# Loading and splitting a guessed first expert's weights during attention

## Chip, core and metric

One core of a Trainium2 chip runs the whole program. The metric is device time in microseconds, the median of three runs of one launch.

## What is computed

Three layers in a row, all in float32. First attention: 4 batches, 8 heads, 576 positions, 64 channels a head; the first four heads see a window of 32, the others every fourth of 128 positions. Its output, seen as 2304 tokens of 512 channels, goes through a layer of 8 experts of which each token takes one (the largest logit, with a bias that depends on the token's modality). Then comes a dense layer with a squared ReLU.

```python
logits = x @ w_gate + modality_bias[modality_id]
e_idx = np.argmax(logits, axis=1)
for e in range(E):
    mask = e_idx == e
    h = np.maximum(x[mask] @ w1[e], 0.0)
    out[mask] = gate_w[mask, None] * (h @ w2[e])
...
h = np.maximum(x @ w_in, 0.0)
return h * h @ w_out
```

w1 is 512 x 1024 and w2 1024 x 512 for each expert, 2 MB each.

## The kernel before

**Attention** runs in 48 units of 96 queries and four heads (`schedule`, the loop over i). A unit passes through steps in several rounds of the loop: A (line 321) writes a mask and the scores into one of PSUM banks 0 to 2 (lines 335, 338) and VectorE (DVE) takes the maximum; C takes the exponential on ScalarE (ACT, line 350); two rounds later D transposes (line 360) and ACT copies (pt); one round later F multiplies by v (line 374), DVE makes x, and SyncE's queue (SP) stores it to the DRAM tensor xd; two rounds later H transposes x (line 413), and ACT and DVE split it into a high and a low part (xth, xtl). After twelve units, one batch is done: its gate logits (line 434) and `route` and `select`, some sixty small DVE operations that count tokens per expert, are threaded into the following rounds as the generator `side`, step by step.

**Experts** run in slots of 128 tokens of one expert (`Moe`). Every float32 product is made of three TensorE (PE) products of rounded parts (float32r): high by high, high by low, low by high. So weights have to be split: ACT copies the staged weights st into the high part (w1h, w2h) and DVE subtracts for the low part (w1l, w2l). A slot j has `begin` (load its expert number and flag into registers, gather its tokens from xd by Pool), `tx` (four transposes into the bank that l1 uses next, xh and xl), `l1` (24 matmuls of 128x512), `th` (eight transposes of the hidden layer, hth and htl) and `l2` (24 matmuls). `main(j)` issues l1(j), then prep(j + 1) if that slot has begun, then l2(j - 1), then th(j). From slot 1 on, loading (line 708) and splitting (line 727) are conditional: they happen only where a slot's expert differs from that of the slot before. Slot 0 loads and splits always (lines 710 and 722 to 726); Pool does two of its w1 subtractions, and the w2 split is threaded into its l1.

**What sets the order.** `slots(0, 6)` is a filler: each round of the attention loop takes three microseconds' worth of steps by nominal costs from it, and a step that yields a negative number ends a round's share. `ready` is how many slots have been selected: 2 after batch 1, 6 after batch 2, all after batch 3 (`WAVES`). If slot j has not been prepared when its turn comes, the filler passes six times (2 x `GAP`, two a round) before it prepares it. The order within an engine is the order of issue; engines wait for each other by semaphores. After slot 5 the rest of the slots run with the decoding of the dense layer's weights beside them, then the dense layer.

Line 785 of the changed kernel is 761 of this one (l1), 815 is 791 (l2), 798 is 774 (th), 771 is 747 (tx), 451 is 434, 468 is 451, 430 is 413, 377 is 360, 391 is 374, 352 and 355 are 335 and 338, 750 is 727.

Of the kernel before, what the change touches and what calls it, by code (L numbers as in the profile page):

```python
# [63 lines left out]
@with_exitstack  # L64
def body(ctx, tc, ins, out):
    nc = tc.nc
    const = ctx.enter_context(tc.tile_pool(name="const", bufs=1))
    dram = ctx.enter_context(tc.tile_pool(name="dram", bufs=1, space=bass.MemoryType.DRAM))
    psum = ctx.enter_context(tc.tile_pool(name="psum", bufs=1, space=PSUM))
    g = Ctx()  # L70
    g.tc, g.nc, g.ins, g.out = tc, nc, ins, out
    g.xd = dram.tile([NT, XW], F32, name="xd")
    g.ya = dram.tile([NA * 128, XW], F32, name="ya")
    g.yb = dram.tile([NT - NA * 128 + 128, XW], F32, name="yb")
    g.wod = [dram.tile([NE, 128, DM], F32, name=f"wo{i}") for i in range(2)]
    g.bk = [psum.tile([128, 512], F32, name=f"bk{i}") for i in range(8)]
    g.ident = const.tile([128, 128], F32, name="ident")
    g.iota = const.tile([128, NCOL], F32, name="iota")
    g.esel = const.tile([1, 4, NSLOT], I32, name="esel")
    g.nsl = const.tile([1, 1], I32, name="nsl")  # L80

    with ExitStack() as mctx:
        moe = Moe(g, mctx)
        with ExitStack() as actx:
            att = Attention(g, actx)
            att.warm(9)
            with tc.manual_schedule():
                schedule(g, att, moe)
        ffn = Ffn(g, ctx)
        with tc.manual_schedule():  # L90
            for cost in moe.slots(NA, NTT):
                if cost == MARK:
                    ffn.side()
            ffn.rest()
            moe.extras()
            moe.tag()
            ffn.l1(0, 0)
            ffn.l1(0, 1)
            run(moe.l2(NSLOT - 1))
        mctx.close()  # L100
        ffn.run()
# [6 lines left out]
def run(steps):  # L108
    for _ in steps:
        pass  # L110


def schedule(g, att, moe):
    nu = B * UPB
    moe.banks((2, 4), (4, 2), (2, 2), (7, 7))
    side, fc, sc, hold, nxt, due = None, 0.0, 0.0, 0, 0, 0
    early = None
    i = 0
    fill, more = moe.slots(0, NA), True

    def step(cost):
        nonlocal side, sc, hold
        if i < hold:
            return
        sc += cost
        while side is not None and sc > 0 and i >= hold:
            c = next(side, None)
            if c is None:
                side = None
            elif c == 0:  # L130
                hold, sc = i + 1, 0.0
            else:
                sc -= c
        sc = min(sc, 0.0)

    def one():
        step(0.01 - sc)

    def filler(cost, late):
        nonlocal more, fc  # L140
        fc += cost
        while more and fc > 0:
            c = next(fill, None)
            if c is None:
                more = False
            elif c == -2 and late:
                fc = max(fc, BURST)
            elif c < 0:
                fc = 0.0
            else:  # L150
                fc -= c
                if early and c == MARK:
                    early.step()
        fc = min(fc, 0.0)

    for i in itertools.count():
        att.tail = i >= nu + 2
        ns, no, nh = (2, (5,), (5,)) if att.tail else (2, (5,), (6,)) if moe.ready else (3, (5, 4), (7,))
        r = RATE2 if i >= nu + 5 else RATE1 if moe.prepped else RATE
        if i == nu + 6:  # L160
            att.units.close()
            early = Early(g)
        if i == nu + 2:
            moe.banks((2, 4), (6, 0), (1, 1), (7, 3))
        att.A(i, (0, 1, 2)[:ns])
        if i == SETUP:
            att.setup()
        if NTL < i <= nu + 5 and i % NTL == 5:
            att.logits(i // NTL - 1, 1)
            if moe.ready and not att.tail:  # L170
                no, nh = nh, no
        if i > hold:
            step(r)
        att.H(i - 5, nh)
        filler(FILL / 2, False)
        att.D(i - 2)
        step(r)
        att.F(i - 3, no, one)
        att.C(i)
        filler(FILL / 2, True)  # L180
        step(r)
        if NTL < i <= nu + 5 and i % NTL == 4:
            att.logits(i // NTL - 1, 0)
        if due and side is None:
            moe.ready = sum(WAVES[due - 1])
            moe.pump()
            due = 0
        if nxt < B and side is None and i >= (nxt + 1) * UPB + 5:
            side = att.batch(nxt)
            due, sc, hold = nxt, 0.0, i + 1  # L190
            nxt += 1
        if not more:
            break
    run(side or ())
    early.close()
    if due:
        moe.ready = NSLOT
        moe.pump()


class Attention:
    def __init__(self, g, ctx):
# [25 lines left out]
        self.reset = al.tile([QT, E, TPB], F32, name="reset")  # L228
        self.taken = al.tile([1, E], F32, name="taken")
        self.pref = al.tile([QT, E], F32, name="pref")  # L230
        self.tok = al.tile([QT, TPB], F32, name="tok")
        self.tbl = al.tile([128, NCOL], F32, name="tbl")
        self.g.itab = None
# [22 lines left out]
    def setup(self):  # L256
        g, nc, ac = self.g, self.g.nc, self.ac
        wraw, mb, modi = self.raw
        nc.gpsimd.memset(self.reset, 1.0)
        nc.gpsimd.memset(self.reset[:, :, 0:1], 0.0)  # L260
        nc.gpsimd.memset(self.tbl, 0.0)
        nc.vector.memset(self.ones, 1.0)
        nc.vector.tensor_copy(self.wg[:, :, 0:E], wraw)
        nc.vector.tensor_tensor(out=self.wg[:, :, E:], in0=wraw, in1=self.wg[:, :, 0:E].bitcast(F32), op=ALU.subtract)
        nc.vector.tensor_scalar(out=self.carry, in0=g.iota[:QT, :E], scalar1=float(128 * NTT), scalar2=None, op0=ALU.mult)
        nc.vector.tensor_scalar(out=self.taken, in0=g.iota[0:1, :E], scalar1=float(NTT), scalar2=None, op0=ALU.mult)
        nc.vector.tensor_scalar(out=self.pref, in0=g.iota[:QT, :E], scalar1=-1.0, scalar2=8.0, op0=ALU.mult, op1=ALU.add)
        modf = ac.tile([QT, NI], F32, name="modf")
        nmod = ac.tile([QT, NI], F32, name="nmod")
        btmp = ac.tile([QT, NI, E], F32, name="btmp")  # L270
        nc.vector.tensor_copy(modf, modi[:, :, 0])
        nc.vector.tensor_scalar(out=nmod, in0=modf, scalar1=-1.0, scalar2=1.0, op0=ALU.mult, op1=ALU.add)
        for j, m, t in ((0, nmod, self.bias), (1, modf, btmp)):
            nc.vector.tensor_tensor(
                out=t, in0=mb[:, j:j + 1, :].to_broadcast([QT, NI, E]),
                in1=m.unsqueeze(2).to_broadcast([QT, NI, E]), op=ALU.mult)
        nc.vector.tensor_tensor(out=self.bias, in0=self.bias, in1=btmp, op=ALU.add)

    def bank(self):
        return self.g.bk[5 if self.tail else 6]  # L280
# [292 lines left out]
    def select(self, j0, n):  # L573
# [35 lines left out]
        ef = new([1, NSLOT + 1], "sef")  # L609
        if j0 == 0:  # L610
            yield 0.12
            nc.vector.memset(ef[:, 0:1], -1.0)
        else:
            yield 0.12
            nc.vector.tensor_copy(ef[:, 0:1], self.elast)
# [56 lines left out]
class Moe:  # L672
# [29 lines left out]
    def stage(self, j, w):  # L702
# [1 line left out]
        e, c = self.chg[j][:2]  # L704
        src = self.g.ins["w1" if w == 0 else "w2"]
        src = src[bass.ds(e, 1)].rearrange("o p c f -> p (o c) f")
        if j:
            nc.sync.dma_start(out=self.st[w], in_=src, cond=c, cond_hint=False)
        else:
            nc.sync.dma_start(out=self.st[w], in_=src)  # L710

    def split(self, j, w):
        nc, tc = self.g.nc, self.g.tc
# [1 line left out]
        src, hi, lo = self.st[w], self.wh[w], self.wl[w]  # L715
        n = src.shape[1]

        def part(k, eng=nc.vector):
            nc.scalar.activation(out=hi[:, k, :], in_=src[:, k, :], func=AF.Copy)
            eng.tensor_tensor(out=lo[:, k, :], in0=src[:, k, :], in1=hi[:, k, :].bitcast(F32), op=ALU.subtract)  # L720

        if j == 0:
            for k in range(n):
                part(k, nc.gpsimd if w == 0 and k < 2 else nc.vector)
                yield -1
            return
        with tc.If(c > 0, preferred_fallthrough_block=False):  # L727
            for k in range(n):
                part(k)

    def begin(self, j):
        nc, g = self.g.nc, self.g
# [80 lines left out]
    def prep(self, j):  # L813
# [1 line left out]
        self.prepped = j + 1  # L815
        yield 0.5
        yield -2
        yield from self.split(j, 0)
        self.done[0] = j + 1
        self.pump()  # L820

# [3 lines left out]
    def main(self, j):  # L825
        if j:
            self.tag()
        self.pump()
        w2 = self.split(0, 1) if j == 0 else iter(())
        for c in self.l1(j):  # L830
            next(w2, None)
            yield c
        if self.begun > j + 1:
            yield from self.prep(j + 1)
        yield 0
# [1 line left out]
            yield from self.l2(j - 1)  # L837
        yield from self.th(j)
        yield -2
        yield from self.split(j, 1) if j else w2  # L840
        self.done[1] = j + 1
        self.pump()
        yield 0
# [316 lines left out]
```

## Time and profile before

| | us |
|---|---|
| runs: median (lowest, highest) | 802.98 (801.03, 803.93) |
| the profiled execution, its span | 803.79, 802.0 |
| PE busy, share of the span | 778.8, 97% |
| DVE, ACT, Pool busy | 412.3, 324.5, 168.5 |
| mean granted clock of PE | 0.991 |

A busy PE is not PE at its peak: how fast it goes is read from the distance between the starts of its instructions, and the granted clock tells whether it ran at 2.4 GHz (1.0) or at 1.2 (0.5). The stages in the order of time: attention to about 120 us, its last units with the first slots to about 160, expert slots to about 385, the dense layer to the end. Of the rows below, those of the stretches (busy time of each engine, granted clock, DMA) tell where PE has holes, those in the order of time what each hole waits for.

### The profile page before, as it was taken

How to read it: one execution, taken by the hardware profiler on the slowest of the kernel's cores; microseconds unless marked ns; L12 is line 12 of the kernel's file. 1: busy time of each engine (PE TensorE's matmuls, PEld its weight loads, DVE VectorE, ACT ScalarE, POOL GpSimd, SP SyncE). 2: the span in 40 equal slices, each digit the busy share in tenths (PEclk: the TensorE clock that was granted, in tenths of full speed). 3: DMA queues.
4: the chain of work that ended last, by engine and by line, in shares of the span. 5: the costliest groups of instructions: out<-in, count | busy, mean ns of one | idle time of the engine just before them, and what ended most of it. 6: DMA issues, size and time to landing. Idle time of an engine off the chain costs nothing.

```text
span 802.0 us, 12644 instructions
## 1 busy us (share of the span) xinstructions
PE 778.8 (97%) x4273; PEld 671.3 (84%) x4273; DVE 412.3 (51%) x1136; ACT 324.5 (40%) x779; POOL 168.5 (21%) x222
## 2 busy tenths in 40 slices
PE   8999987999899999999899999999999999999996
PEld 5888875778688888878888899899899998998995
DVE  5787888566447777443279832333243233234232
ACT  4877766333445455543244522322232232232221
POOL 4245632224413333301033510010010001001001
PEclk9999998999999999999999999999999999999999
DMA  7676672234534444361355310010010001001001
GB/s 220 186 166 174 183 256 81 73 93 134 155 108 132 119 134 143 133 198 35 118 167 146 105 40 27 4 50 27 1 52 1 27 14 40 1 0 40 1 1 39
DMA packets 49130, 72.65 MB, mean 91 GB/s; under 512 B 7296, under 2 KB 31712, under 8 KB 48544
## 3 DMA queue, kind: packets, MB, share of 16 engines
q1 hardware_dynamic: 43040, 56.00, 24.1%
q0 software_dynamic: 3280, 10.76, 4.5%
q10 hardware_dynamic: 2736, 4.99, 1.7%
q8 instruction: 35, 0.57, 0.3%
q14 instruction: 39, 0.32, 0.1%
HBM read 132.27 MB, written 17.06 MB: 186 GB/s over the span
## 4 chain that ended last, share of the span: by engine, by line
issue 39%; PE 10%; POOL 2%; POOLq 0%; DVE 0%; ACT 0%; ACTq 0%
PE bk L1010 5%; PE bk L1064 4%; POOL out L1069 2%; PE bk L791 1%; PE bk L993 0%; POOLq L1156 0%; DVE fsq L1020 0%; ACT fr L1018 0%; POOLq L1069 0%; ACTq L1018 0%
## 5 line engine op out<-in xcount | busy, mean ns | idle before, releaser
L1020 DVE TENSOR_TENSOR fsq<-fr 128x384 f32<-128x384 f32 x96 | 53.4, 556 | 162.8 <-ACT fr L1018 162.3
L1010 PE MATMUL bk<-yh,wih 128*128 128x384 f32 x384 | 130.0, 339 | 2.1 <-ACTq L860 1.5
L1010 PE MATMUL bk<-yh,wil 128*128 128x384 f32 x384 | 129.2, 336 | 0.0
L1010 PE MATMUL bk<-yl,wih 128*128 128x384 f32 x384 | 129.0, 336 | 0.0
L1018 ACT ACTIVATE fr<-bk 128x384 f32<-128x384 f32 x96 | 46.9, 488 | 192.0 <-PE bk L1010 191.4
L1064 PE MATMUL bk<-woh,fhh 128*128 128x512 f32 x288 | 113.2, 393 | 0.0
L1064 PE MATMUL bk<-woh,fhl 128*128 128x512 f32 x288 | 112.8, 392 | 0.0
L1064 PE MATMUL bk<-wol,fhh 128*128 128x512 f32 x288 | 112.6, 391 | 0.0
L1069 POOL DMA_INDIRECT out<-fout,fidx x18 | 17.6, 978 | 320.8 <-DVE fout L1068 320.2
L1029 DVE TENSOR_TENSOR fhl<-fsq,fhh 128x384 fp32r<-128x384 f32 x96 | 55.3, 576 | 44.2 <-ACT fhh L1028 44.0
L1010 PEld LDWEIGHTS bk<-yh,wih 128*128 128x128 f32 x384 | 72.2, 188 | 4.8 <-ACTq L860 1.8
L1010 PEld LDWEIGHTS bk<-yl,wih 128*128 128x128 f32 x384 | 72.2, 188 | 1.8
L1010 PEld LDWEIGHTS bk<-yh,wil 128*128 128x128 f32 x384 | 72.2, 188 | 0.0
L1028 ACT ACTIVATE fhh<-fsq 128x384 fp32r<-128x384 f32 x96 | 50.3, 524 | 50.9 <-DVE fsq L1020 50.8
L1064 PEld LDWEIGHTS bk<-woh,fhl 128*128 128x128 f32 x288 | 54.0, 188 | 12.3
L761 PE MATMUL bk<-w1h,xh 128*128 128x512 f32 x152 | 63.4, 417 | 0.8 <-DVE htl L777 0.8
L791 PE MATMUL bk<-w2h,hth 128*128 128x512 f32 x152 | 61.6, 405 | 1.9 <-ACTq L727 1.9
L1064 PEld LDWEIGHTS bk<-wol,fhh 128*128 128x128 f32 x288 | 54.1, 188 | 9.6
L1064 PEld LDWEIGHTS bk<-woh,fhh 128*128 128x128 f32 x288 | 54.1, 188 | 9.5
L761 PE MATMUL bk<-w1l,xh 128*128 128x512 f32 x152 | 61.0, 401 | 0.4 <-DVEq L727 0.4
L761 PE MATMUL bk<-w1h,xl 128*128 128x512 f32 x152 | 60.9, 401 | 0.0
L791 PE MATMUL bk<-w2l,hth 128*128 128x512 f32 x152 | 60.0, 395 | 0.4 <-DVEq L727 0.4
(174 smaller groups left out, 1360.1 us busy)
## 6 DMA issues: line engine op xcount, KB each, us to landing
st<-in_w SPq DMA_DIRECT2D x41, 2048.0 KB
raw<-in_wi SPq DMA_DIRECT2D x32, 256.0 KB
raw<-in_wo SPq DMA_DIRECT2D x32, 256.0 KB
v<-in_v SPq DMA_DIRECT2D x7, 780.0 KB
q<-in_q SPq DMA_DIRECT2D x7, 576.0 KB
kd<-in_k SPq DMA_DIRECT2D x14, 288.0 KB
xd<-x SPq DMA_DIRECT2D x40, 96.0 KB
yb<-y ACTq DMA_DIRECT2D x13, 256.5 KB
```

Source lines behind the costliest of these rows:

```text
L761: nc.tensor.matmul(ps, a[:, c, :], w[:, c, sl], start=k == 0, stop=k == 11)
L791: nc.tensor.matmul(ps, a[:, c, :], w[:, c, :], start=k == 0, stop=k == 23)
L1010: nc.tensor.matmul(ps, w[:, c, f * 128:(f + 1) * 128], a[:, c, :], start=k == 0, stop=k == 11)
L1018: nc.scalar.activation(out=r, in_=ps, func=AF.Relu)
L1020: nc.vector.tensor_tensor(out=s, in0=r, in1=r, op=ALU.mult)
L1028: nc.scalar.activation(out=hh, in_=s, func=AF.Copy)
L1029: nc.vector.tensor_tensor(out=hl, in0=s, in1=hh.bitcast(F32), op=ALU.subtract)
L1064: nc.tensor.matmul(acc[t], a[:, sl], w[:, f, :], start=f == 0 and j == 0, stop=f == NF - 1 and j == 2)
L1069: dma = nc.gpsimd.indirect_dma_start(out=out, out_offset=bass.IndirectOffsetOnAxis(ap=self.idx[:, i:i + 1].bitcast(U32), axis=0), in_=o, i ...
```

## The change

Before attention starts, `setup` makes a guess at slot 0's expert: it marks each modality's largest bias, and takes the lower-numbered of the marked experts (`g.guess`, eight small DVE operations). A generator `first` then loads that expert's w1 and w2 in sixteen pieces of 128 x 512 (256 KB each) by SP; each piece is split two steps later by ACT and DVE into w1h and w1l, w2h and w2l. The attention loop takes a step of it in every second round from round 4, and in each round after the 24th, while no routing step is due. With round 34 it is through. `select` compares slot 0's expert with the guess instead of with -1; loading and splitting of slot 0 are now conditional like those of the others, and the always-path with Pool's two subtractions and the threaded w2 split is gone.

```diff
@@ schedule
+    first = moe.first()
@@
+        if i > SETUP and (side is None or i < hold) and (i % 2 == 0 or i > 2 * UPB):
+            next(first, None)
         if due and side is None:
+            run(first)
             moe.ready = sum(WAVES[due - 1])
             moe.pump()
@@ setup
+        nc.vector.tensor_reduce(out=top, in_=mb[0:1], axis=AX.X, op=ALU.max)
+        nc.vector.tensor_tensor(out=at, in0=mb[0:1], in1=top.to_broadcast([1, 2, E]), op=ALU.is_equal)
+        nc.vector.tensor_tensor(out=at[:, 0], in0=at[:, 0], in1=at[:, 1], op=ALU.max)
+        nc.vector.tensor_tensor_scan(out=cum, data0=at[:, 0], data1=at[:, 0], initial=0.0, op0=ALU.add, op1=ALU.bypass)
+        nc.vector.tensor_scalar(out=at[:, 1], in0=cum, scalar1=0.5, scalar2=None, op0=ALU.is_lt)
+        nc.vector.tensor_reduce(out=self.first, in_=at[:, 1], axis=AX.X, op=ALU.add)
+        nc.vector.tensor_scalar(out=self.first, in0=self.first, scalar1=float(E - 1), scalar2=None, op0=ALU.min)
+        nc.vector.tensor_copy(g.guess, self.first)
@@ select
-            nc.vector.memset(ef[:, 0:1], -1.0)
+            nc.vector.tensor_copy(ef[:, 0:1], self.first)
@@ stage
-        if j:
-            nc.sync.dma_start(out=self.st[w], in_=src, cond=c, cond_hint=False)
-        else:
-            nc.sync.dma_start(out=self.st[w], in_=src)
+        nc.sync.dma_start(out=self.st[w], in_=src, cond=c, cond_hint=False)
+
+    def first(self):
+        nc, ins = self.g.nc, self.g.ins
+        e = nc.values_load(self.g.guess[0:1, 0:1], engines=(ET.SP,), min_val=0, max_val=E - 1)
+        parts = []
+        for w in range(2):
+            st, hi, lo = (x[w].rearrange("p c f -> p (c f)") for x in (self.st, self.wh, self.wl))
+            src = ins["w1" if w == 0 else "w2"][bass.ds(e, 1)].rearrange("o p c f -> p (o c f)")
+            for k in range(8):
+                parts.append([x[:, k * 512:(k + 1) * 512] for x in (st, src, hi, lo)])
+        for i in range(len(parts) + 2):
+            if i < len(parts):
+                nc.sync.dma_start(out=parts[i][0], in_=parts[i][1])
+            if i > 1:
+                st, _, hi, lo = parts[i - 2]
+                nc.scalar.activation(out=hi, in_=st, func=AF.Copy)
+                nc.vector.tensor_tensor(out=lo, in0=st, in1=hi.bitcast(F32), op=ALU.subtract)
+            yield
@@ split
-        if j == 0:
-            for k in range(n):
-                part(k, nc.gpsimd if w == 0 and k < 2 else nc.vector)
-                yield -1
-            return
         with tc.If(c > 0, preferred_fallthrough_block=False):
             for k in range(n):
-                part(k)
+                nc.scalar.activation(out=hi[:, k, :], in_=src[:, k, :], func=AF.Copy)
+                nc.vector.tensor_tensor(out=lo[:, k, :], in0=src[:, k, :], in1=hi[:, k, :].bitcast(F32), op=ALU.subtract)
@@ main
-        w2 = self.split(0, 1) if j == 0 else iter(())
-        for c in self.l1(j):
-            next(w2, None)
-            yield c
+        yield from self.l1(j)
```

The first place is PE behind slot 0's transposes (gx), some three units before attention's scores end. `ident,p` is D, `v,pt` is F, `mask` and `kd,q` are A, `ident,x` is H, `w1h,xh` begins l1. Before:

```order
L747 MATMUL bk_70<-ident,gx_92 128x128 x4
L360 MATMUL bk_71<-ident,p 128x96 x4
L374 MATMUL bk_73<-v,pt 96x65 x4
L335 LDWEIGHTS mask
L335 MATMUL bk_68<-mask 96x512
L338 MATMUL bk_68<-kd_145,q 96x256 x2
L413 MATMUL bk_74<-ident,x 128x96 x2
...
L335 MATMUL bk_69<-mask 96x512
...
L761 MATMUL bk_70<-w1h,xh 128x512
```

Two units of attention stand between the transposes and l1. And on PE in the changed kernel, from the same transposes on:

```order
L771 MATMUL bk_70<-ident,gx_93 128x128 x4
L377 MATMUL bk_71<-ident,p 128x96 x4
L391 MATMUL bk_73<-v,pt 96x65 x4
L750 UNCONDITIONAL_BRANCH
L785 MATMUL bk_70<-w1h,xh 128x512
L785 MATMUL bk_70<-w1l,xh 128x512
L785 MATMUL bk_70<-w1h,xl 128x512
...
L352 LDWEIGHTS mask
L352 MATMUL bk_68<-mask 96x512
```

Nine l1 matmuls moved ahead of the two units, right behind the conditional block.

The second place is PE between the end of l2 of slot 0 and l1 of slot 2, where batch 3's logits (`xth,wg`) and routing transposes (`ident,lt`) come in. Before, the logits stand in l2 and slot 2's transposes are long done:

```order
L434 MATMUL bk_73<-xtl,wg 16x288
L791 MATMUL bk_75<-w2h,hth 128x512
L791 MATMUL bk_75<-w2l,hth 128x512
L791 MATMUL bk_75<-w2h,htl 128x512
L774 MATMUL bk_74<-ident,hr 128x128 x4
L774 MATMUL bk_68<-ident,hr 128x128 x4
L761 MATMUL bk_70<-w1h,xh 128x512
```

On PE in the changed kernel the two last H, the logits, the routing transposes and slot 2's own transposes (gx) stand one behind the other in this place:

```order
L815 MATMUL bk_75<-w2h,htl 128x512
L798 MATMUL bk_74<-ident,hr 128x128 x4
L430 MATMUL bk_73<-ident,x 128x96 x2
L798 MATMUL bk_68<-ident,hr 128x128 x4
L430 MATMUL bk_73<-ident,x 128x96 x2
L750 UNCONDITIONAL_BRANCH
L451 MATMUL bk_73<-xth,wg 16x288
...
L468 MATMUL bk_73<-ident,lt 96x16 x6
L771 MATMUL bk_69<-ident,gx_95 128x128 x4
L750 UNCONDITIONAL_BRANCH
L785 MATMUL bk_70<-w1h,xh 128x512
```

Slot 2's transposes moved from ahead of l2(0) to behind the routing transposes, and no l2 or l1 matmul stands among these rows.

The third place is DVE behind slot 0's transposes in the changed kernel (xl is the low part of its tokens, rpo to rci are routing of batch 2, x is of F):

```order
L773 TENSOR_TENSOR xl<-bk_70,xh 128x512
L774 COPY row_103<-gx_93 128x1
L775 COPY row_103<-sc_100 128x1
L525 TENSOR_TENSOR rpo<-rpo,rwit 96x48
...
L536 TENSOR_SCALAR rci<-rpos 96x6
L400 TENSOR_TENSOR x<-bk_73,rc 96x256
L750 COMPARE_AND_BRANCH
```

The block's branch stands behind routing operations and x; before, there was no branch, and the subtractions of w1 stood among the following units' operations.

## Rows read from the trace of the kernel before

**Rows 1.** Busy time by stretch (us from the start; engines, PE's clock, DMA share, GB/s).

```profile
20.00:100.00 80.00, 80.00 (x687) 68.42 (x686) 62.97 (x219) 61.45 (x204) 36.99 (x54) 1.00 0.70 177
...
117.00:163.00 46.00, 38.83 (x238) 30.57 (x236) 32.81 (x111) 23.31 (x55) 9.34 (x10) 0.93 0.31 98
...
200.00:216.00 16.00, 13.01 (x53) 9.70 (x53) 7.88 (x21) 6.36 (x14) 6.63 (x11) 0.89 0.55 176
```

**Rows 2.** PE in order of time, one unit (start, us, instruction, [idle before <-releaser]).

```profile
96.81 0.82 PE L374 MATMUL bk<-v,pt 128*96 128x65 f32 x8
97.46 0.38 PE L335 MATMUL bk<-mask 96*96 96x512 bf16 x1
...
98.55 0.33 PE L413 MATMUL bk<-ident,x 96*128 96x96 f32 x2
98.72 0.49 PE L360 MATMUL bk<-ident,p 96*128 96x96 f32 x4
99.04 0.54 PE L550 MATMUL bk<-rval,rhot 96*128 96x144 f16 x6
```

**Rows 3.** PE in order of time, from slot 0's transposes to its first l1 matmuls.

```profile
117.35 0.60 PE L747 MATMUL bk<-ident,gx 128*128 128x128 f32 x4
...
127.48 1.54 PE L374 MATMUL bk<-v,pt 128*96 128x65 f32 x8 [3.05 <-DVE x L383]
128.78 0.77 PE L761 MATMUL bk<-w1h,xh 128*128 128x512 f32 x1
...
132.34 0.58 PE L761 MATMUL bk<-w1h,xl 128*128 128x512 f32 x1
```

**Rows 4.** DVE, then Pool, in order of time, in the same stretch.

```profile
120.51 0.42 DVE L383 TENSOR_TENSOR x<-bk,rc 96x256 f32<-96x256 f32 x1
...
121.59 1.81 DVE L526 CAST rrf<-rri 96x6 f32<-96x6 int32 x1
...
123.59 2.19 DVE L537 TENSOR_SCALAR rhot<-iota,rrf 96x128 f16<-96x128 f32 x1
...
121.02 4.68 POOL L720 TENSOR_TENSOR w1l<-st,w1h 128x1024 fp32r<-128x1024 f32 x2 [10.28 <-ACT w1h L719]
```

**Rows 5.** PE in order of time, up to slot 2's first l1 matmuls.

```profile
160.84 0.32 PE L434 MATMUL bk<-xth,wg 128*16 128x288 f32 x1 [0.54 <-DVE lt L438]
161.00 0.32 PE L434 MATMUL bk<-xtl,wg 128*16 128x288 f32 x1
...
162.16 1.03 PE L774 MATMUL bk<-ident,hr 128*128 128x128 f32 x8
162.95 0.48 PE L761 MATMUL bk<-w1h,xh 128*128 128x512 f32 x1
163.27 0.40 PE L761 MATMUL bk<-w1l,xh 128*128 128x512 f32 x1
163.50 0.40 PE L761 MATMUL bk<-w1h,xl 128*128 128x512 f32 x1
```

**Rows 6.** DVE, then ACT, in order of time: links of the chain to l1.

```profile
112.40 0.20 DVE L454 TENSOR_TENSOR lg<-bk,bias 96x48 f32<-96x48 f32 x1 [0.55 <-PE bk L451]
...
165.82 0.15 DVE L823 COPY y<-lrow 128x1 f32<-128x1 f32 x1 [0.34 <-DVEq L727]
...
171.74 0.18 DVE L495 COPY rtin<-rtot 96x48 f32<-96x48 f32 x1 [0.34 <-DVEq L727]
...
113.35 0.24 ACT L464 ACTIVATE rex<-rd 96x48 f32<-96x48 f32 x1 [1.35 <-DVE rd L461]
...
169.96 0.60 ACT L748 ACTIVATE xh<-bk 128x512 fp32r<-128x512 f32 x1
```

**Rows 7.** Instructions on st (count: duration ns min/median/max, first and last start, forms).

```profile
L719 ACT ACTIVATE w2h<-st x16: 618/627/644, 130.7 to 362.4; 128x512 fp32r<-128x512 f32 x16
L720 DVE TENSOR_TENSOR w2l<-st,w2h x16: 670/676/692, 132.6 to 363.9; 128x512 fp32r<-128x512 f32 x16
```

**Rows 8.** Busy time by stretch, five microseconds of attention.

```profile
70.00:75.00 5.00, 5.00 (x43) 4.26 (x42) 3.75 (x13) 3.82 (x14) 3.97 (x6) 1.00 0.98 225
```

**Rows 9.** PE in order of time, in front of slot 4's l2.

```profile
210.80 0.50 PE L791 MATMUL bk<-w2h,hth 128*128 128x512 f32 x1 [1.92 <-ACTq L727]
```

More of the change, by code (lines that the diff above doesn't have):

```diff
@@ L80, in body @@
     g.nsl = const.tile([1, 1], I32, name="nsl")
+    g.guess = const.tile([1, 1], I32, name="guess")
     with ExitStack() as mctx:
@@ L230, in __init__ @@
         self.pref = al.tile([QT, E], F32, name="pref")
+        self.first = al.tile([1, 16], F32, name="gfirst")[:, :1]
         self.tok = al.tile([QT, TPB], F32, name="tok")
@@ L277, in setup @@
         nc.vector.tensor_tensor(out=self.bias, in0=self.bias, in1=btmp, op=ALU.add)
+        top = ac.tile([1, 2, 1], F32, name="gtop")
+        at = ac.tile([1, 2, E], F32, name="gat")
+        cum = ac.tile([1, E], F32, name="gcum")
+        nc.vector.tensor_reduce(out=top, in_=mb[0:1], axis=AX.X, op=ALU.max)
[6 more added lines that the diff above has]
+        nc.vector.tensor_copy(g.guess, self.first)
     def bank(self):
@@ L716, in split @@
         n = src.shape[1]
-        def part(k, eng=nc.vector):
-            nc.scalar.activation(out=hi[:, k, :], in_=src[:, k, :], func=AF.Copy)
-            eng.tensor_tensor(out=lo[:, k, :], in0=src[:, k, :], in1=hi[:, k, :].bitcast(F32), op=ALU.subtract)
-        if j == 0:
-            for k in range(n):
-                part(k, nc.gpsimd if w == 0 and k < 2 else nc.vector)
-                yield -1
-            return
         with tc.If(c > 0, preferred_fallthrough_block=False):
             for k in range(n):
-                part(k)
+                nc.scalar.activation(out=hi[:, k, :], in_=src[:, k, :], func=AF.Copy)
+                nc.vector.tensor_tensor(out=lo[:, k, :], in0=src[:, k, :], in1=hi[:, k, :].bitcast(F32), op=ALU.subtract)
     def begin(self, j):
@@ L817, in prep @@
         yield -2
-        yield from self.split(j, 0)
+        self.split(j, 0)
         self.done[0] = j + 1
@@ L839, in main @@
         yield -2
-        yield from self.split(j, 1) if j else w2
+        self.split(j, 1)
         self.done[1] = j + 1
```

## The prediction

> **What bounds the kernel now.** I read first the busy time by stage, then the order in time of TensorE (PE) in the stage that the change touches, then what the other engines did where PE waited. PE is the bound nearly everywhere: from 20 to 100 us, in attention, it is busy all 80 us, while DVE is busy for 62.97 and ACT for 61.45 [rows 1]. Its order there shows why: one attention unit costs PE 0.65 us (line 374), 1.09 (lines 335 and 338), 0.17 (line 413) and 0.32 (line 360), 2.23 us from start to start, with no gap [rows 2]. So work that moves into attention finds no free PE time; only holes on PE can be won. The change touches one stage with holes: from 117 to 163 us PE is busy for 38.83 of 46 us, at a mean granted clock of 0.93 [rows 1].
>
> **How much is lost there.** Both kernels do the same PE work between the first slot's transposes at 117.35 and slot 2's first matmul at 162.95 [rows 3, 5]: 45.6 us. Start-to-start times give the work: 48 l1 matmuls at 0.235 (163.27 to 163.50 in [rows 5]) 11.3; 24 l2 matmuls at 0.23 5.5; three score steps at 1.09 3.3; eight line-413 pairs at 0.17 1.4; six line-360 groups at 0.32 1.9; seven line-374 groups at 0.65 4.6; 16 logits matmuls at 0.155 [rows 5] 2.5; 28 transposes of 128x128 at 0.1 (162.16 to 162.95 is eight) 2.8; the table matmuls 0.4 [rows 2]. Sum 33.7, so 11.9 us are lost. The largest piece is the 3.05 us before 127.48, where PE waits for DVE's x; after it the clock is at 1.2 GHz, and eight matmuls take 3.56 us (128.78 to 132.34) where 0.235 each would be 1.9 [rows 3]; with the line-374 group that took 1.3 instead of 0.65 the slow clock costs 2.3. DVE is late for three reasons: routing of batch 2, the split of slot 0's weights, and two long waits while Pool does 4.68 us of that split: a 96x6 cast took 1.81 us and a 96x128 compare 2.19 [rows 4].
>
> **The change, part by part.**
> Taken away: Pool's two subtractions, ACT's four and DVE's two of w1, and the w2 split in l1(0), from this stage; the two 2 MB loads ahead of it too. That opens the way for slot 0's matmuls at once, and the order shows them two attention units earlier. The guess is right on this data: worked out from the reference's inputs, both modalities favour expert 1, and 989 of the first 1152 tokens go to it, so slot 0 is expert 1 and its conditional loads and splits are skipped.
>
> Added in attention: 16 ACT copies at 0.627 and 16 DVE subtractions at 0.676 [rows 7], and 16 loads of 256 KB on SP's queue. A unit needs 61.45/80 x 2.23 = 1.71 us of ACT and 1.76 of DVE. With a piece every second unit that is 2.03 and 2.09 a unit: under PE's 2.23, so it is hidden. Over units 24 to 30 there is a piece in each: DVE 2.43, over by 0.2 a unit, 1.4 in seven. Queued behind a piece on ACT and DVE stand the copies and subtractions that free PE's banks, so a backlog reaches PE when it passes about one unit's slack. The loads: DMA queues are busy 0.70 of 20 to 100 us, but 0.98 of 70 to 75, at 225 GB/s [rows 1, 8]. At that rate a piece takes 1.2 us, so a few pieces behind a q, k or v load come a microsecond or two late, and ACT, which takes its instructions in order, waits. Bounds for the whole: 0 (all hidden) and 3 us (the 1.4 plus one late load). I take 1.0, nearer to hidden since ACT and DVE idle over a fifth of the stage. The eight small operations on DVE in setup (0.2 each, as line 454 in [rows 6]) are 0 to 1.6 us; DVE has idle time there, so I take 0. The sixteen issues on SP stand between x stores and q, k, v loads; the stores have six buffers: 0.
>
> Added at slot 0: the first l1 matmuls now stand right behind transposes, line 360 and line 374, ahead of the next score step (the first pair of order listings). PE is through those at 117.35 + 0.4 + 0.32 + 0.65 = 118.7. The split is now a conditional block; the low half counts as written only when DVE has passed it, and in DVE's order it stands behind routing and x. That x ends at 120.93 [rows 4]; passing a skipped block took 0.34 [rows 6]. So PE waits to 121.3, less one matmul that it may issue: 2.4 lost. From there the remaining 29.3 us of work run interleaved with attention, so that ACT and DVE keep up; I allow 1.2 for waits like the 0.54 for the logits in [rows 5]. The l1 of slots 0 and 1 and l2(0) are then done at 121.3 + 29.3 + 1.2 = 151.8.
>
> Added behind it, a hole: in the old order slot 2's transposes and l1 lead on from l2(0), with logits in the middle of it. In the new one the two last attention transposes, batch 3's logits and routing transposes stand between th(1) and slot 2's transposes, and no filler is left (the filler pauses for six steps when slot 2 was not ready in time). It is a chain through ACT and DVE. From the start of th to DVE behind the w2 block took 162.16 to 165.82 = 3.66 [rows 5, 6]; one more xtl (0.34) stands in it now: 4.0. Then xtl 0.34; four logits 0.62; their addition, 0.7 until PE goes on (0.54 idle and the last one's tail); four more 0.62; addition 0.7; six transposes 0.4: 7.4. From routing's first addition to the end of its exponential took 112.40 to 113.59 = 1.2, and ACT's xh stands behind that: 8.6. From xh to DVE behind the block took 169.96 to 171.74 = 1.8 [rows 6]. Sum 10.4 us, with 3.2 of PE work in it and one matmul that may go ahead: 7.0 lost. Slot 2's l1 runs from 161.9.
>
> Clock: the second hole is three times as long as the one that dropped it before, so I charge the same 2.3 behind it, and 0.5 for the first (2.4 us idle, about one chance in five). That makes 164.7. The old kernel was at 162.95, plus 0.4 for the six transposes that it does later: 163.35. So the stage loses **1.35 us**; with the 1.0 in attention the whole loses **2.4 us**. All later work is in the same order but for a step, and I charge nothing. The profiled execution took 803.79 us, 802.0 of it the span, 0.8 above the median of 802.98; 803.8 + 2.4 = 806.2, and from the median **805.4**.
>
> **Rivals.**
> *Faster.* Slot 5's hole goes as well. Near 208 PE waits 1.92 us for ACT [rows 9], which there waits for a store of decoded weights; 200 to 216 us holds 3.0 us of idle PE and a clock of 0.89 [rows 1], together 4.5 lost. The decoding runs one step earlier against the slots now. If that frees it, and the clock costs nothing in the first hole and half behind the second (1.65 less): 805.4 - 4.5 - 1.65 = 799.2, and with nothing lost in attention 798.2, which is the time of this case. Against: the store still stands behind the same conditional load on SP in the order. 0.15.
>
> *Slower: loads starve ACT.* If pieces behind q, k and v land over two units (4.5 us) after their issue, ACT stops on each in units 24 to 30, and with it all that PE needs. From 65 to 75 us five pieces at 1.2 are added to DMA queues that are nearly full; that is up to 6 us of backlog, and PE loses what passes half a unit of slack (1.1 us, an estimate: a bank that ACT empties is written again one unit later): 6 less 1.1, or 5 more than I charged without it, 810.4. It decides from the point where a piece takes over 4.5 + 1.1 = 5.6 us. The Trainium skill ("DMA: Bandwidth & Descriptors", section Bandwidth) says the same as a rule: "Batch DMAs to ≥1 MiB for ≥75% of peak", which speaks against cutting 2 MB into eight. Its fit (section "Anatomy of one DMA — SWDGE (gpsimd) path", 2.0 us + bytes/436e3) gives 2.6 us for a piece alone, an estimate by which none is late and the result would be 804.4; no run here shows a piece yet. 0.23.
>
> *Slower: the second hole is longer*, because slot 2's rows are gathered late or DVE has more routing ahead of it: each microsecond is one on the path; with 3 more, 808.4. 0.10.
>
> *The change doesn't do what it says*: the guess is wrong, 4 MB are loaded again, and the splits (w1 and w2, 10 us of ACT) stand before l1(0): about 812. The inputs speak against it. 0.02.
>
> **How the numbers follow.** 0.5% (4.0 us) is about what a measurement of this kernel can tell from no change. The forecast, 0.50, lies within it, 799.0 to 807.0. Faster by more has 0.15; slower by more 0.23 + 0.10 + 0.02 = 0.35. The range takes in attention's 0 to 3, the 2.8 of clock either way, and both main rivals' prices: 798.5 to 811.0, with about 0.2 left out.
>
> **What would show it.** Right: slot 0's l1 some eight us earlier; PE idle some 2 us before it, then dense to about 152; then a stretch of some 10 us with 3 us of work, ended by DVE behind line 750, with half the clock behind it; the attention units still at 2.23. Wrong: the second stretch under 5 us (then faster), units 24 to 30 spread out with ACT waiting for st (then slower), or slot 0's block taken.

## The result, and the profile after

| | before | after |
|---|---|---|
| median of four runs, us (lowest, highest) | 802.97 (801.03, 803.93) | 814.16 (812.12, 814.75) |
| profiled execution, its span, us | 803.79, 802.0 | 814.12, 812.3 |
| mean granted clock of PE | 0.991 | 0.985 |

The changed kernel is slower: ratio 1.0122, interval 1.0095 to 1.015. By the ratio that is 9.8 us (7.6 to 12.0), by the medians of the table 11.2. The prediction had 2.4, and its range ended at 811.0.

The loss is where the prediction had charged one microsecond. The busy time by stretch of the changed kernel, in the order attention, from slot 0's transposes to slot 2's l1, the stretch behind it, and the place of slot 5's old hole, which was at 200 to 216 before and stands 14.3 us later here, as slot 5's transposes do (columns as in [rows 1]):

```profile
20.00:100.00 80.00, 74.23 (x590) 59.70 (x589) 62.66 (x211) 58.91 (x190) 29.27 (x42) 0.96 0.77 203
...
130.00:174.50 44.50, 37.96 (x242) 29.62 (x239) 23.87 (x105) 17.14 (x46) 3.48 (x6) 0.92 0.19 53
174.50:183.60 9.10, 9.01 (x26) 6.71 (x27) 3.46 (x19) 0.60 (x1) 1.15 (x2) 0.63 0.33 69
...
214.30:230.30 16.00, 14.63 (x70) 11.33 (x69) 7.18 (x20) 6.95 (x15) 4.86 (x7) 1.00 0.53 172
```

In attention PE was busy for all 80 us [rows 1]; now it has holes, though DVE's busy time is the same and ACT's is less. Counted by the mask matmul that opens a unit: unit 40 (counted from 0) starts at 102.33 before and at 115.00 after. From there on the new kernel is the faster one. From unit 40 to slot 0's transposes 15.0 us pass in both; from these to slot 2's l1 45.6 before and 44.5 after; to slot 3's transposes 6.3 and 9.1, at the clock of 0.63 above; to slot 7's transposes 55.6 and 52.8, where PE's idle time in the row of slot 5's hole is 1.4 us instead of 3.0 and the clock stays at 1.00 instead of 0.89; to the end 577.1 and 575.9. Sum: 12.7 - 1.1 + 2.8 - 2.8 - 1.2 = 10.4, the difference of the two spans (812.35 less 802.00).

How a unit is stretched is read from ACT's, DVE's and SP's order in time around one of them (start, us, engine, line, operation, [idle before <-releaser]; L367 is the exponential, L358 the maximum, L740 and L741 the two halves of a split, L737 the piece's load):

```profile
70.33 1.13 ACT L367 ACTIVATE p<-bk,nm 96x128 f32<-96x128 f32 x4 [0.71 <-DVE nm L358]
71.35 0.63 ACT L740 ACTIVATE w2h<-st 128x512 fp32r<-128x512 f32 x1
...
73.39 1.13 ACT L367 ACTIVATE p<-bk,nm 96x128 f32<-96x128 f32 x4 [0.82 <-DVE nm L358]
75.70 0.63 ACT L740 ACTIVATE w2h<-st 128x512 fp32r<-128x512 f32 x1 [1.18 <-DMA st<-in_w]
...
72.01 0.69 DVE L741 TENSOR_TENSOR w2l<-st,w2h 128x512 fp32r<-128x512 f32 x1 [0.77 <-ACT w2h L740]
72.62 0.68 DVE L358 TENSOR_REDUCE nm<-bk 96x4 f32<-96x512 f32 x1
...
70.25 0.36 SPq L737 DMA_DIRECT2D st<-in_w  x1
```

This is a ring. The copy on ACT stands behind the exponential (1.02 us from start to start), DVE's subtraction waits for the copy (0.66), the next unit's maximum stands behind the subtraction in DVE's order (0.61), and the next exponential waits for that maximum (0.77): 3.06 us, where PE needs 2.23. Neither engine is full; each waits for the other once in a turn. The same from the waits of ACT and of DVE from 20 to 115 us (engine, line, waited for: us in total, times, longest):

```profile
ACT p L367 <- DVE nm L358: 9.8, 13, 1.0
...
ACT w2h L740 <- DMA st<-in_w: 1.2, 1, 1.2
...
ACT w1h L740 <- DMA st<-in_w: 0.4, 1, 0.4
...
DVE w1l L741 <- ACT w1h L740: 6.6, 8, 1.1
DVE w2l L741 <- ACT w2h L740: 6.5, 7, 1.9
```

In the kernel before, ACT never waited for a maximum (nm) in that stretch. The other cost stands in the row at 75.70: one piece, issued at 70.25 behind loads of q and k, is not there when ACT comes to it. (The 0.4 us are another piece, issued at 41.98; its copy starts 4.4 us later.) On PE, in order of time:

```profile
74.82 0.38 PE L352 MATMUL bk<-mask 96*96 96x512 bf16 x1
75.04 1.03 PE L355 MATMUL bk<-kd,q 128*96 128x256 f32 x4
77.97 0.39 PE L430 MATMUL bk<-ident,x 96*128 96x96 f32 x2 [1.90 <-DVE xtl L434]
...
81.03 0.42 PE L451 MATMUL bk<-xtl,wg 128*16 128x288 f32 x1 [0.95 <-DVE xtl L434]
...
81.73 0.63 PE L352 MATMUL bk<-mask 96*96 96x512 bf16 x1
```

This unit, number 28, takes 6.91 us; in the next, of 4.63 us, the mask matmul takes 0.63 instead of 0.38, at the low clock.

### The profile page after: what moved, and what is told of

Same layout as the page of the kernel before. It is cut to its first block, busy times and chain, and to the rows that moved or that the text cites. A ratio compares the mean times of both kernels' runs of the same rounds, so it can differ in the third digit from the quotient of the medians.

```text
span 812.3 us, 12740 instructions
## 1 busy us (share of the span) xinstructions
PE 782.5 (96%) x4273; PEld 672.2 (83%) x4273; DVE 412.1 (51%) x1150; ACT 324.1 (40%) x783; POOL 167.2 (21%) x220
## 4 chain that ended last, share of the span: by engine, by line
issue 40%; DVE 4%; POOL 2%; DMA 2%; PE 1%; ACT 1%; SPq 0%; POOLq 0%; ACTq 0%; DVEq 0%
POOL out L1090 2%; DVE fhl L1050 1%; DMA raw<-in_wo 1%; DVE da L913 1%; DVE da L919 1%; PE bk L815 1%; DVE da L908 1%; DMA yb<-y 1%; DVE fsq L1041 1%; PE bk L1031 1%; POOL wol L924 0%; ACT fhh L1049 0%; DVE da L916 0%; ACT dm L906 0%; SPq L1071 0%
## 5 line engine op out<-in xcount | busy, mean ns | idle before, releaser
L367 ACT ACTIVATE p<-bk,nm 96x128 f32<-96x128 f32 x192 | 54.0, 363 | 21.4 <-DVE nm L358 15.2
```

The costliest lines, as they stand in the source:

```text
L367: self.g.nc.scalar.activation(out=p[:, h, :], in_=ps[:, h, :], func=AF.Exp, bias=nm[:, h:h + 1], scale=1.0)
```

## Experiments

Three explanations stood against each other: the ring, the late load, and simply too much work on ACT and DVE in the rounds that have a piece each (after the 24th). The measure common to all is the time from the start of unit 7 to that of unit 38, which leaves the program's start out: 20.80 to 97.46 before, 76.66 us; 21.00 to 110.13 after, 89.13, which is 12.5 more. How exact it is shows in two kernels further down (GAP = 1 and 4) that have the changed kernel's program up to unit 38: they take 90.4 and 88.9. Times are given against the kernel before on the same chip.

**The subtraction one step later.**

```diff
...
-            if i > 1:
+            if 2 <= i < len(parts) + 2:
                 st, _, hi, lo = parts[i - 2]
                 nc.scalar.activation(out=hi, in_=st, func=AF.Copy)
+            if i >= 3:
+                st, _, hi, lo = parts[i - 3]
                 nc.vector.tensor_tensor(out=lo, in0=st, in1=hi.bitcast(F32), op=ALU.subtract)
```

> Each piece's subtraction on DVE is issued one step later than its copy on ACT; loads and copies stay where they are. Theory 1 (a ring across engines: exponential, the piece's copy behind it on ACT, the subtraction that waits for it on DVE, the next maximum behind that, the next exponential; 1.0 + 0.65 + 0.6 + 0.8 = 3.05 us where PE needs 2.23): the ring is cut, DVE no longer idles in front of a subtraction, unit 40 starts at 105 to 108 us (before 102.3, changed kernel 115.0), the whole takes 804 to 808 us. Theory 2 (late loads: ACT waits for a piece and everything behind it stops): nothing of it is touched, unit 40 stays at 113 to 115, the whole at 811 to 814. Theory 3 (ACT and DVE have too much to do in the rounds with a piece each): unchanged too, 811 to 814.

809.77 against 804.66, ratio 1.0076 (1.0058 to 1.0094). Unit 40 at 110.0, between what ring and load foretold; units 7 to 38 take 83.33, 5.8 less than after. DVE no longer waits for a copy at all, and ACT hardly for a maximum, but the late load weighs more. ACT's waits, 20 to 115 us:

```profile
ACT w2h L740 <- DMA st<-in_w: 3.7, 1, 3.7
...
ACT p L367 <- DVE nm L358: 1.2, 3, 0.6
```

**A longer lead.** The split comes four steps after the load (`parts[i - 4]`, copy and subtraction together).

> Each piece is split four steps after its load instead of two; copy and subtraction stay side by side. Theory 2 (late loads): the one wait for a load (1.2 us on ACT, 1.9 on PE, and the slow clock behind it) goes and with it most of the loss: unit 40 at 104 to 106 us, the whole at 803 to 806. Theory 1 (the ring): the ring is still there, only that wait and the clock behind it go: unit 40 at 109 to 112, the whole at 808 to 811.

812.43, ratio 1.0113 (1.0092 to 1.0133). Unit 40 starts at 114.1, later than either theory said; in part because the last two copies move to 104.9 and 108.0, where units 37 and 38 take 1.0 more than after. Units 7 to 38 take 87.84, only 1.3 less than after. No wait for st is left; the ring is whole, in the waits of ACT and of DVE:

```profile
ACT p L367 <- DVE nm L358: 10.6, 13, 0.9
...
DVE w2l L743 <- ACT w2h L740: 5.4, 7, 1.0
DVE w1l L743 <- ACT w1h L740: 5.1, 7, 1.3
```

**No loads.**

```diff
         for i in range(len(parts) + 2):
-            if i < len(parts):
-                nc.sync.dma_start(out=parts[i][0], in_=parts[i][1])
+            if i in (0, 5):
+                nc.gpsimd.memset(self.st[i // 5], 0.01)
```

> The sixteen piece loads are left out, st holds a constant that Pool writes in rounds 4 and 14, and the splits stay where they are, so slots that go to the guessed expert compute with that constant. Theory 1 (the ring): units 20 to 36 are still spread to 2.6 to 3.2 us where they have a piece; unit 40 starts at 108 to 111 us and the whole takes 807 to 811. Theory 2 (late loads, or loads that hold up q, k and v): unit 40 is back at 102.3 to 104, the whole at 801 to 804.

813.41, ratio 1.0104 (1.0056 to 1.0151): slower than foretold by either; 1.7 us of it stand ahead of unit 7 in the profiled execution. Units 7 to 38, on PE:

```profile
22.49 0.38 PE L352 MATMUL bk<-mask 96*96 96x512 bf16 x1
...
108.69 0.38 PE L352 MATMUL bk<-mask 96*96 96x512 bf16 x1
```

86.20 us, 9.5 more than before with no load in it: the splits in their order cost that. It is 2.9 less than after, 3.3 less in units 28 and 29 alone, and the clock stays at 1.00 there.

**Loads alone.** The loads stay in their rounds; all sixteen splits come in one block before slots 0 and 1 are released.

```diff
...
+        while not self.flush:
+            yield
+        for st, _, hi, lo in parts:
+            nc.scalar.activation(out=hi, in_=st, func=AF.Copy)
+            nc.vector.tensor_tensor(out=lo, in0=st, in1=hi.bitcast(F32), op=ALU.subtract)
```

> The sixteen loads stay in their rounds, all sixteen copies and subtractions come in one block just before the first slots are released (round 40). Up to unit 40 only the loads can cost. Theory 1 (the ring): unit 40 starts within 1 us of 102.3. Theory 2 in the form that the loads hold up q, k and v loads or x stores: unit 40 at 105 or later. Behind it the block of 16 x 0.68 us on DVE is in the way of everything, so the whole takes 808 to 815 under either.

815.46, ratio 1.0153 (1.0114 to 1.0193). Two unit starts and then the block, on PE:

```profile
21.52 0.38 PE L353 MATMUL bk<-mask 96*96 96x512 bf16 x1
...
98.15 0.38 PE L353 MATMUL bk<-mask 96*96 96x512 bf16 x1
...
118.74 1.54 PE L392 MATMUL bk<-v,pt 128*96 128x65 f32 x8 [9.22 <-DVE lt L456]
```

76.63 us for units 7 to 38, the 76.66 of before. Sixteen loads of 256 KB cost nothing by themselves: they hold up neither q, k and v nor the stores of x. They cost only where ACT's order makes everything wait for one. (Unit 40 starts at 103.4, just outside what the theory said; 0.7 us of it stand ahead of unit 7.)

**Lead and late subtraction together** (copy at `i - 4`, subtraction at `i - 5`).

> Both edits together: a piece is copied four steps after its load and subtracted one step later still. If ring and late load are two separate costs, the 2.5 us hole near 75 us that was left with the later subtraction goes, with the slow clock behind it: unit 40 at 105 to 107 us (110.0 with the later subtraction alone, 114.1 with the longer lead alone), the whole 1 to 3 us above the kernel before. If what is left there is DVE's work in rounds with a piece each (theory 3), unit 40 stays at 109 to 110 and the whole 4 to 5 above.

807.91 against 804.72, ratio 1.0052 (1.0026 to 1.0078). Units 7 to 38 take 79.40, 2.7 over before. With the two single edits this is a table of two by two: 89.1 with neither, 83.3 with the later subtraction, 87.8 with the longer lead, 79.4 with both. Together the edits take away 9.7, but ring and late load are not two costs that add up: the later subtraction takes 5.8 with the short lead and 8.4 with the long one, the lead 1.3 and 3.9.

The reason is in units 28 and 29, which took 5.7 us before, at a granted clock of 1.00: 11.5 after (0.70), 10.1 with the later subtraction (0.83), 9.5 with the lead (0.82), 5.9 with both (1.00). Either the ring or the late load is enough for holes here, and mostly for a slow clock behind them (in the kernel without loads these two units took 8.3 at 1.00). In the other 29 units the later subtraction takes 4.4 and 4.8, and the lead nothing. So the ring is 5.8 to 8.4, and 6.8 by the kernel without loads; the late load with what follows on it is 1.3 to 3.9, and 2.9 by that kernel. The 1.3 is no more than kernels of the same program differ by. With both gone, 2.7 are left.

Unit 40 starts only at 110.58, for a new reason: PE waits for routing's table operands from Pool. Pool and DVE there, and PE, in order of time:

```profile
95.83 0.84 POOL L555 TENSOR_SCALAR rval<-iota,rcf,tok 96x144 f16<-96x144 f32 x1
...
99.25 1.67 POOL L555 TENSOR_SCALAR rval<-iota,rcf,tok 96x144 f16<-96x144 f32 x1
...
99.52 0.68 DVE L743 TENSOR_TENSOR w2l<-st,w2h 128x512 fp32r<-128x512 f32 x1
...
104.62 0.22 PE L567 MATMUL bk<-rval,rhot 96*128 96x144 f16 x1 [1.19 <-POOL rval L555]
106.03 0.28 PE L567 MATMUL bk<-rval,rhot 96*128 96x144 f16 x1 [1.19 <-POOL rval L555]
```

Three of Pool's operations take 1.44, 1.67 and 1.67 instead of 0.84, each with a subtraction in its span.

**Every second round throughout**, with the subtraction one step later and the lead of two. The step is not taken in each round after the 24th, and what is left of w2 is split up to slot 0's block for it.

```diff
-        if i > SETUP and (side is None or i < hold) and (i % 2 == 0 or i > 2 * UPB):
+        if i > SETUP and (side is None or i < hold) and i % 2 == 0:
...
-            run(first)
...
+        if j == 0:
+            run(self.rest)
         self.split(j, 1)
```

> On top of the later subtraction (lead of two steps): a step in every second round throughout, also after the 24th; the last pieces, of w2, are then split in rounds 40 to 47 and the rest in front of slot 0's own block for w2. Theory 3 (what is left is ACT and DVE over PE's pace where each round has a piece): unit 40 at 103 to 104.5, and the whole from 2 below to 1 above the kernel before, as the stages behind attention are 1.5 to 2.6 shorter than its. If pieces cost wherever they stand, unit 40 is still at 106 or later, or the loss turns up in rounds 40 to 47.

805.33, ratio 0.9998 (0.9976 to 1.0021): the loss is gone, and no gain in its place. Unit 40 at 104.6; units 7 to 38 take 78.75, 2.1 over before. That spreading helps is not shown by the 0.6 that this is below the 2.7: the five kernels of this pace, alike up to unit 38, take 78.0 to 79.2 there, and only 13 of the 16 copies and 12 of the 16 subtractions fall into these units. Too much work in consecutive rounds is a small part at most. Behind unit 40 it takes 701.4 us to the end where the changed kernel takes 697.3, though the profiled execution, 807.78, is the slowest of ten. Of these 4.1, 1.3 are between slot 0's transposes and slot 2's l1, and 1.8 between that and slot 7's transposes, where slot 5's hole is back (PE waits 1.6 for ACT in front of slot 4's l2).

**The pause.** Five kernels change `GAP`, the pause of the filler, to take the second hole away: the changed kernel with 1 and with 4, and the even pace with 1, 4 and 5; a sixth keeps 3 for slot 0 and takes 1 for slot 2.

```diff
-                for _ in range(2 * GAP):
+                for _ in range(2 * (GAP if j == 0 else 1)):
```

> The changed kernel with GAP = 1: the filler pauses for one round instead of three where a slot was not ready, so slot 0 begins two rounds earlier and slot 2 is prepared before batch 3's logits, with attention and logits beside its l1. Theory (the second hole is the chain of logits and routing with no slot's matmuls beside it): the holes between th(1) and slot 2's l1, 7 us in sum with the 1.2 GHz clock behind them, shrink to 1 to 3, and the whole is 3 to 7 us below the changed kernel. Rival (slot 2's rows are gathered too late for that): PE waits for the gather in their place, and the time stays within 2 us of the changed kernel or rises.

> The even pace with the later subtraction, and GAP = 1. If attention's loss and the second hole are separate, the gains add: 4 to 8 us below the kernel before. If the rounds in which slot 0 now begins are those in which the last pieces of w2 are split, DVE and ACT hold up l1(0): no better than the even pace alone.

830.36, ratio 1.0311 (1.0269 to 1.0354), and 817.26, ratio 1.0136 (1.009 to 1.0183). That is 16 and 12 us more than with a pause of three rounds (814.16 and 805.33), which no theory had. The second hole did not go: in front of slot 2's l1 PE waits 3.53, 0.81 and 0.73 us. Another hole came in front of slot 6, whose rows depend on batch 3's routing. PE of the changed kernel with GAP = 1:

```profile
172.47 0.48 PE L430 MATMUL bk<-ident,x 96*128 96x96 f32 x2 [3.53 <-DVE x L400]
...
237.10 1.12 PE L771 MATMUL bk<-ident,gx 128*128 128x128 f32 x4 [6.62 <-DMA gx<-xd,sc]
```

> The changed kernel itself with GAP = 4 and nothing else: attention loses its 12 us as it does, and only the pause differs. Theory (pause): 4 to 8 us below the changed kernel, 3 to 7 above the kernel before. Rival: within 2 us of the changed kernel.

> The even pace with the later subtraction, and GAP = 4: the filler pauses four rounds, so slot 0 is prepared one round later, slot 1's main part comes to its end after slots 2 to 5 are known, and prepares slot 2 itself, without a second pause. Theory (the second hole is a pause that the order makes, since slots 0 and 1 now run out too early): the holes of 8 us in front of slot 2's l1 and the slow clock behind them go, the later start costs about one round (3 us), and the whole is 3 to 8 us below the kernel before. Rival (only the end of batch 3's routing counts, and slots done early wait there): a hole appears in front of slot 6, as it did with GAP = 1, or PE is filled with slots while routing goes on no sooner, and the time stays within 2 us of the kernel before.

821.14, ratio 1.0208 (1.0174 to 1.0241), and 808.23, ratio 1.0047 (1.0027 to 1.0067): worse too. PE of the changed kernel with GAP = 4, and its stretch from 150 to 180 us (columns as in [rows 1]):

```profile
168.10 1.12 PE L771 MATMUL bk<-ident,gx 128*128 128x128 f32 x4 [3.43 <-DMA gx<-xd,sc]
...
150.00:180.00 30.00, 24.51 (x119) 19.89 (x119) 10.07 (x51) 7.36 (x18) 4.63 (x8) 0.77 0.20 54
```

Slot 2's transposes now stand in the order before its rows have landed. The clock is low over the whole stretch, ahead of that hole (0.78 from 150 to 168.1) as behind it (0.77 to 180). So the pause of three rounds was not idle: it covered the gathering.

> As the one with GAP = 4, with a pause of five rounds: slots 0 to 2 then begin in the rounds in which they begin in the kernel before. What is left of the change is that their weights are there. Theory: the stage from slot 0's transposes to slot 2's l1 still loses less than before (no waits for the split; 11.9 us lost there before), no second hole, the whole 2 to 6 us below the kernel before. Rival (PE only waits for something else there, slots 0's gather or routing): within 2 us of the kernel before.

804.2, ratio 1.0000 (0.998 to 1.0021), the rival's result. Slot 2's transposes are at 154.5, as before (154.1), though slot 0's come 7.4 us later than before: from slot 0's transposes to slot 2's l1 it takes 38.7 where before took 45.6, so the weights do save 6.9 us in this stage, and the later start gives it back.

> The even pace with the later subtraction; the pause stays three rounds for slot 0 and is one round for slot 2. Slot 2 is prepared two rounds sooner and its l1 stands beside the last attention steps and batch 3's logits. Theory (pause): the holes in front of slot 2's l1 shrink from 8 to under 3 us, the whole 3 to 8 us below the kernel before. Rival (end of batch 3's routing): a hole of 4 us or more in front of slot 6, no gain.

802.77 against 804.75, ratio 0.9976 (0.9956 to 0.9996): the one kernel of the thirteen whose interval lies below the old one, by 0.24%, less than the theory's 3 to 8 us; with so many tried, and an upper end this near to 1, the gain is not firm. No hole of the rival's size stands in front of slot 6. Slot 2's l1 in the two kernels of the even pace: first the shorter pause, its PE and the ten microseconds from l1's start, then those with the pause of three rounds.

```profile
158.28 0.39 PE L429 MATMUL bk<-ident,x 96*128 96x96 f32 x2 [2.12 <-DVE xtl L433]
158.51 0.60 PE L772 MATMUL bk<-ident,gx 128*128 128x128 f32 x4
159.84 0.49 PE L786 MATMUL bk<-w1h,xh 128*128 128x512 f32 x1 [0.73 <-ACTq L751]
...
159.84:169.84 10.00, 9.10 (x39) 6.15 (x39) 1.80 (x6) 1.05 (x2) 1.16 (x2) 0.83 0.28 79
```

```profile
165.81:175.81 10.00, 9.93 (x33) 7.54 (x34) 3.44 (x19) 1.52 (x3) 1.15 (x2) 0.69 0.37 71
```

The wait of 2.12 us is still there, but l1 stands ahead of the logits: it starts 40.5 us after slot 0's transposes instead of 45.8. The clock falls behind it in both, to 0.83 and 0.69. The two profiled executions differ by 6.5 us, the medians by 2.6, so the rows show where time is won and not how much.

## Why the prediction was wrong

**The step that failed** is the charge for sixteen pieces in attention: 1.0 us with bounds of 0 and 3, where 12.7 were lost. It compared each engine's work per unit (ACT 2.03, DVE 2.09, up to 2.43) with PE's 2.23 and took what is below as hidden. That counts throughput, and left out that the two halves of one split lie on two in-order engines with a unit's exponential and maximum between them; a chain through both is longer than either engine's work. The prediction's own text names the link (the copies and subtractions that free PE's banks are queued behind a piece), but follows it on each engine alone. Measured over units 7 to 38: 12.5, of which ring and late load together are 9.7 (the ring 5.8 to 8.4, the load 1.3 to 3.9, depending on which is taken away first) and the rest 2.7. The step's own reason for a loss, too much on DVE in consecutive rounds (1.4), can only be in that rest. Of the prediction's sign for a slower result, units 24 to 30 spread out with ACT waiting for st, the first half came true; ACT waited 13 times for a maximum and twice for st.

**The load.** The prediction's rival had ACT stop on pieces that stand behind q and k, deciding from 5.6 us after issue, with 5 us to pay. It came about twice, with copies starting 4.4 and 5.45 us after the issue, both short of that point and both later than the prediction's estimate for a piece alone; the second of these waits, 1.18 us on ACT, counts. So the mechanism exists. Its price, taken as what goes with the lateness, is 2.9 us with the ring there (the kernel without loads) and 3.9 with the ring cut (the lead), where the rival had 5. The kernel with the loads alone shows that loads as such do not cost, and the even pace that a wait on ACT need not: there ACT waits 2.14 us for a piece at 47.66, and that unit and the two behind it are together 0.2 longer than before. What counts is where the wait stands.

**What held.** The guess is right, and slot 0's conditional loads and splits are passed. The first hole: from slot 0's transposes at 130.01, l1 starts 2.7 us later and goes on after 3.7 (4.0 foretold). The second hole, from the start of th on:

```profile
164.00 0.60 PE L798 MATMUL bk<-ident,hr 128*128 128x128 f32 x4
...
167.33 0.43 PE L430 MATMUL bk<-ident,x 96*128 96x96 f32 x2 [2.12 <-DVE xtl L434]
168.71 0.42 PE L451 MATMUL bk<-xth,wg 128*16 128x288 f32 x1 [0.94 <-DVE xtl L434]
...
170.39 0.42 PE L451 MATMUL bk<-xth,wg 128*16 128x288 f32 x1 [0.54 <-DVE lt L455]
...
172.07 0.66 PE L468 MATMUL bk<-ident,lt 16*96 16x16 f32 x6 [0.54 <-DVE lt L455]
...
174.53 0.79 PE L785 MATMUL bk<-w1h,xh 128*128 128x512 f32 x1 [0.76 <-ACTq L750]
```

10.5 us from start to l1, where the sum of links gave 10.4, and 44.5 from slot 0's transposes to slot 2's l1, where it gave 44.5 (161.9 less 117.35). The clock behind it is under-charged: from slot 2's l1 to slot 3's transposes it takes 9.1 us where before took 6.3, of which 0.4 are six transposes that now stand ahead, so 3.2 for 2.3. From slot 0's transposes to slot 3's the change loses 1.7 us, where the sum gave 1.35. The way these links were added, row by row through both engines, is what the attention term lacked.

**The rival on the faster side** came true in part: the stretch with slot 5's hole shrank by 2.8 of the 4.5 us named, and cannot be seen in a total that attention had already lost. It is not a fixed gain: from slot 3's transposes to slot 7's, 52.8 us here, it took 53.7 in the kernel with the later subtraction and 54.8 at the even pace, so it differs from kernel to kernel; that it hangs on how the decoding meets the slots is likely but not shown. The 1.2 us behind slot 7's transposes are within what the kernels differ by there (575.4 to 577.8). **A longer second hole** and **a wrong guess** did not occur.

**What stays open.** Of the 16 and 7 us that a pause of one and of four rounds cost in the changed kernel, the rows show where holes appear (6.6 and 3.4 us for gathered rows) and the low clock around them, not a full account. By stages, with one round: 5.9 less from unit 40 to slot 0's transposes, 7.3 more to slot 2's l1, 12.5 more to slot 7's transposes; with four rounds 1.9, 2.2 and 1.7 more, and 1.9 behind. The 2.1 us that pieces cost at the even pace, and the 2.7 with both edits, were not taken apart either.

## What to carry to other kernels

Work that is to hide on half-idle engines has to be followed as a chain, not summed: list what the new instruction waits for and what stands behind it on its queue, go round until the chain comes back to a step of the loop, and compare that length with the period. Where it is longer, issue the second half of a two-engine step a round later, so that it never waits; here this alone took away 5.8 of the 12.5 us in attention. A load that feeds an in-order engine needs a lead that covers whatever is ahead of it on its queue, and a hole that is closed on one side should be looked for on the other, since here a pause of one round added a hole without closing the first, one of four rounds put another in its place, and one of five closed it and gave the time back by a later start.

## What the runs showed of the hardware

Loads in sixteen quarter-megabyte pieces were free: 76.63 us for units 7 to 38 with them, 76.66 without. The rule of the Trainium skill for large transfers ("DMA: Bandwidth & Descriptors", section Bandwidth) was quoted against them in the prediction; in this stage, with the DMA queues busy for 0.87 of the time from 20 to 100 us, no cost of it shows.

Pool's operation on 96x144 elements went from 0.84 us to 1.44 and 1.67 where DVE's subtraction of two SBUF tensors fell into it, by 0.6 to 0.83, about one such subtraction (0.68). The Trainium skill ("SBUF — State Buffer", section "Who interferes with whom") says that a DVE instruction with two SBUF inputs contends with a GpSimd instruction that reads SBUF; these rows agree. It makes the subtraction of a split a cost to Pool as well, 2.3 us over three of them, at a time when PE waits for Pool.

Which of the two gives way differs from kernel to kernel, though Pool's operation starts first in all these rows. In the changed kernel, where the subtraction has waited for its copy, it is the subtraction that takes longer, 0.84 instead of 0.68, and Pool keeps its time:

```profile
100.84 0.85 POOL L555 TENSOR_SCALAR rval<-iota,rcf,tok 96x144 f16<-96x144 f32 x1
...
101.00 0.84 DVE L741 TENSOR_TENSOR w2l<-st,w2h 128x512 fp32r<-128x512 f32 x1 [0.70 <-ACT w2h L740]
```

Why it differs is not shown.
